# Whole-tile PSUM copies in an attention backward pass, and a reordered last stage

## The chip, the cores and the metric

One core of one Trainium2 chip runs the kernel as one program. The metric is the device time of one execution in microseconds (us). Five engines work at once and meet through semaphores: TensorE (PE; its weight loads are PEld), VectorE (DVE), ScalarE (ACT), GpSimd (POOL) and SyncE (SP), whose instructions here are only DMA issues. "SPq", "ACTq" and "POOLq" are the instruction queues of these engines where they issue DMAs or wait. Each queue runs in program order.

## The reference

The forward pass is a parallel block (attention and a gated feed-forward network on the same normalised input); the kernel returns its output and the gradients with respect to six inputs.

```python
def _A_ref(x, wqkv, wo):            # S = 2048, D = 448, H = 16, Dh = 28
    qkv = (x @ wqkv).reshape(B, S, 3, H, Dh).transpose(2, 0, 3, 1, 4)
    q, k, v = qkv[0], qkv[1], qkv[2]
    scores = jnp.einsum("bhqd,bhkd->bhqk", q, k) * (Dh ** -0.5)
    p = _softmax(scores, axis=-1)
    o = jnp.einsum("bhqk,bhkd->bhqd", p, v)
    return o.transpose(0, 2, 1, 3).reshape(B, S, D) @ wo

def _B_ref(x, w_gate, w_up, w_down):          # F = 1792
    return (_silu(x @ w_gate) * (x @ w_up)) @ w_down

x = A_x
xn = _layernorm(x, axis=-1)                   # eps = 1e-5
return x + _A_ref(xn, A_wqkv, A_wo) + _B_ref(xn, B_w_gate, B_w_up, B_w_down)
...
_out, _vjp = jax.vjp(_f, A_x, A_wqkv, A_wo, B_w_gate, B_w_up, B_w_down)
return (out, *_vjp(grad_out))                 # everything in bfloat16
```

## The kernel before

Everything is cut into 16 row tiles of 128 rows (NT = 16). Heads are padded from 28 to 32 and taken in 4 groups of 4 heads (G = 4). The program has four stages, laid out by hand; the order on each engine's queue is the order in which the Python text emits instructions, because the tile framework is told to keep it and adds only the semaphores.

**Prologue and forward stage** (0 to about 730 us): normalisation, projections, attention forward, feed-forward network forward and backward. The change doesn't touch it.

**Backward stage** (lines 777 to 858, about 730 to 1558 us). It walks over 512 units. A unit is one pair of heads (pr, 8 of them), one block of 512 keys (kc, 4), one half of the rows (w, 2) and one tile of 128 rows in that half (qi, 8). Eight units that differ only in qi make a window (UW = 8; W is its number, pos the place in it), and there are 64 windows. Iteration k of the loop does, in this order:

- PE, L798: the scores of unit k into a PSUM tile `sd` (two banks; the pool has three such tiles). PE, L811: the product dO V^T of unit k-1 into the next `sd` tile.
- ACT, L816: E[k] = exp(scores). DVE, L828: ds[k-1] = (L811's result) * E[k-1].
- ds must also be had transposed, in the tile `dsT`, for the gradient of q. For six of eight units SP issues a transposing DMA (L830). For qi = 1 and qi = 4 (TQ) PE transposes instead (`pe_transpose`, L718, eight 128x128 transposes into the PSUM tile `aux`, one bank), and `tr_out` copies the bank out: ACT the first half (L725), DVE the second (L727). The unit with qi = 1 is transposed at the end of pos 6; the one with qi = 4 at pos 0 of the next window, between L798 and L811 (`late_tr`).
- PE, L691 (`acc_mm`): the sums of dV and dK over the units, three units behind.

Spread over each window are: a job of 14 to 21 PE matmuls (the list `jobs`, lines 655 to 662; a few windows have none), emitted in four parts at pos 1 to 4 and copied out by ACT at pos 4 (`job_out`, L670); and the q gradient of two windows ago (`dq_mm`, L740, at pos 5, and `dq_out` on DVE at pos 6, L752 to L758). Transposes, job and `dq_mm` all use the one buffer of `aux`, in turn: each must wait until the one before has been copied out. Loads for later windows are put into the SP queue between the transposing DMAs (`job_load`, `load_pair`, `load_group`, `load_w`); `ds` has eight buffers, and one is free again when its transposing DMA has landed.

**Last stage** (lines 862 to 918, from about 1565 us). `dwq_mms` adds up the weight gradient of head group 3 for four chunks c of 128 input features: 32 K/V matmuls (L619, reading `dkv_sp`), then 32 q matmuls (L624, reading `dq_sp`, which arrives by a transposing DMA that SP issues last). Chunk by chunk, each into its own `sd` tile, and `dwq_out` copies each out (ACT L634, POOL L641 and L642). Then, for each row tile t, PE adds the input gradient g_ps from `pab` (L893, two partial sums of the earlier jobs) and from `dq_c` (L895, 12 matmuls), and the layer norm's backward follows: DVE copies g_ps to SBUF and sums its rows (L899), DVE multiplies it by xn and sums (L903, `junk`), two tiny DVE instructions make the coefficients bb and cc (L907, L909), ACT makes t1 (L912), DVE t2 (L914), POOL adds dy (L917), and SP stores the tile (L918). `load_c` loads `dq_c` two row tiles at a time, three loads ahead; `pab` and `dy_t` are loaded whole before the loop.

Of the kernel before, what the change touches and what calls it, by code (L numbers as in the profile page):

```python
# [18 lines left out]
D = 448  # L19
# [3 lines left out]
G = 4  # L23
# [14 lines left out]
def kernel(  # L38
# [573 lines left out]
    def dwq_mms(g, c, ps):  # L612

        out = []
        lhs = lambda t: xn_sp[:, t, c * P:(c + 1) * P]

        def kvm(t):
            for hp in range(2):
                pe.matmul(ps[:, hp * P:(hp + 1) * P], lhsT=lhs(t), rhs=dsp[2 * g + hp][0][:, t, :],  # L619
                          start=(t == 0 and hp == 0), stop=(t == NT - 1), skip_group_check=True)  # L620

        def qm(t):
            for hp in range(2):
                pe.matmul(ps[:, 256 + hp * 64:256 + hp * 64 + 64], lhsT=lhs(t),  # L624
                          rhs=dsp[2 * g + hp][1][:, t // 8, t % 4, t % 8 // 4, :],
                          start=False, stop=(t == NT - 1), skip_group_check=True)
        for f in (kvm, qm):
            out += [lambda t=t, f=f: f(t) for t in range(NT)]
        return out

    def dwq_out(g, c, ps):
        d0, dn = DCH[c]
        o = outp.tile([P, 384], BF16, name="dwq_raw")
        act.copy(out=o[:], in_=ps[:, :384])  # L634
        z = outp.tile([P, 3, 4, DH], BF16, name="dwq_z")
        kv = o[:, :256].rearrange("p (h v j r) -> p h v j r", h=2, v=2, r=HP)
        for tq in range(3):
            for hp in range(2):
                src = (o[:, 256 + 64 * hp:320 + 64 * hp].rearrange("p (j r) -> p j r", r=HP) if tq == 0
                       else kv[:, hp, 2 - tq])  # L640
                pool.tensor_copy(out=z[:, tq, 2 * hp:2 * hp + 2, :], in_=src[:, :, :DH])  # L641
        pool.dma_start(  # L642
            out=out_2[d0:d0 + dn, :].rearrange("p (t c) -> p t c", t=3)[:, :, g * 4 * DH:(g + 1) * 4 * DH],
            in_=z[:dn].rearrange("p t h d -> p t (h d)"))

    def job_mms(i, ps):
        j = jobs[i]
        if j[0] == "dwq":
            return dwq_mms(j[1], j[2], ps)
        if j[0] == "y":  # L650
# [10 lines left out]
        return [lambda n=n: pe.matmul(ps[:, :D], lhsT=t[:, n, :], rhs=w[:, n, :],  # L661
                                      start=(n == 0), stop=(n == NFC - 1)) for n in range(NFC)]
# [50 lines left out]
    def pe_transpose(W, qi):  # L713

        ds, dsT = DS[W * UW + qi], st[("dsT", W)]
        ps = ps_x.tile([P, 8, P], BF16, name="aux")
        for i in range(8):
            pe.transpose(ps[:, i, :], ds[:, i // 4, (i % 4) * P:(i % 4 + 1) * P], ident_bf[:])  # L718
        st["tr"] = (ps, dsT[:, :, :, qi * P:(qi + 1) * P])

    def tr_out(eng):

        ps, dst = st["tr"]
        if eng is act:
            act.copy(out=dst[:, 0], in_=ps[:, 0:4, :])  # L725
        else:
            dve.tensor_copy(out=dst[:, 1], in_=ps[:, 4:8, :])  # L727

    def dq_mm(W, half):
        pr, kc, w, _ = units[W * UW]  # L730
# [46 lines left out]
    for k in range(N + 2 * UW):  # L777
# [21 lines left out]
                          rhs=kv[HP * j:HP * j + HP, kc * 512:(kc + 1) * 512],  # L799
                          start=True, stop=True, tile_position=(HP * j, 0))  # L800
        late_tr = pos == 0 and 1 <= W <= NW
        if late_tr:
            pe_transpose(W - 1, TQ[1])
        if 1 <= k <= N:
            pr, kc, w, qi = units[k - 1]
            q, kv = qd[pr]
            qt = 8 * w + qi
            d_ps = ps_sd.tile([P, 2, 512], FP32, name="sd")
            for j in range(2):
                r = 64 + HP * j  # L810
                pe.matmul(d_ps[:, j, :], lhsT=q[r:r + HP, qt * P:(qt + 1) * P],  # L811
                          rhs=kv[r:r + HP, kc * 512:(kc + 1) * 512],
                          start=True, stop=True, tile_position=(r, 0))
        if k < N:
            E[k] = ework.tile([P, 2, 512], BF16, name="E")
            act.activation(out=E[k][:], in_=s_ps[:], func=ACT.Exp, scale=SCALE)  # L816
        if late_tr:
            tr_out(act)
            tr_out(dve)
        job = jobs[W] if W < len(jobs) else None  # L820
        if pos == 6 and 2 <= W <= NW + 1:
            dq_out(W - 2)
# [29 lines left out]
            job_out(W, st["aux"])  # L852
        if pos == 6 and W < NW:
            pe_transpose(W, TQ[0])
            tr_out(act)
            tr_out(dve)
    while sp_later:
        sp_later.pop(0)()
# [3 lines left out]
    with ExitStack() as fin:  # L862
# [1 line left out]
        wk = fin.enter_context(tc.tile_pool(name="wk", bufs=3))  # L864
        one = fin.enter_context(tc.tile_pool(name="one", bufs=1))
        dy_t = one.tile([P, NT, D], BF16, name="dy_t")
        act.dma_start(out=dy_t[:], in_=dy_d)
        pab = [one.tile([P, NT, D], BF16, name=f"pab{i}") for i in range(2)]
        for i, src in enumerate((pA_d, pB_d)):
            for hf in range(2):  # L870
                sp.dma_start(out=pab[i][:, 8 * hf:8 * hf + 8, :], in_=src[:, 8 * hf:8 * hf + 8, :])
        dq_c = {}

        def load_c(ck):
            if ck < NT // 2:
                dq_c[ck] = ckf.tile([P, 3 * G, 2 * P], BF16, name="dq_c")
                sp.dma_start(out=dq_c[ck][:], in_=dqkv_d[ck])
        load_c(0)
        load_c(1)
        for c in range(4):  # L880
            ps = ps_sd.tile([P, 2, 512], FP32, name="sd")
            for f in dwq_mms(3, c, ps[:, 0, :]):
                f()
            dwq_out(3, c, ps[:, 0, :])
        wq = wtile["wq"]
        for t in range(NT):
            if t % 2 == 0:
# [6 lines left out]
            for n in range(3 * G):  # L894
                pe.matmul(g_ps, lhsT=cks[:, n, (t % 2) * P:(t % 2 + 1) * P], rhs=wq[:, n, :],  # L895
                          start=False, stop=(n == 3 * G - 1))
            g_sb = wk.tile([P, D], FP32, name="g_sb")
            s1 = wk.tile([P, 1], FP32, name="s1")
            dve.tensor_scalar(out=g_sb[:], in0=g_ps, scalar1=1.0, scalar2=None, op0=ALU.mult, op1=ALU.add,  # L899
                              accum_out=s1[:])  # L900
            junk = wk.tile([P, D], FP32, name="junk")
            s2 = wk.tile([P, 1], FP32, name="s2")
            dve.scalar_tensor_tensor(out=junk[:], in0=g_sb[:], scalar=1.0, in1=xn_sp[:, t, :D],  # L903
                                     op0=ALU.mult, op1=ALU.mult, accum_out=s2[:])
            bb = wk.tile([P, 1], FP32, name="bb")
            cc = wk.tile([P, 1], FP32, name="cc")
# [43 lines left out]
```

## Time and profile before

| what | value |
|---|---|
| time, median of 3 runs | 1656.14 us (1640.88 to 1673.39) |
| the profiled execution | 1655.46 us, its span 1653.5 us |
| mean granted TensorE clock in it | 0.957 |
| busy: PE / DVE / ACT / POOL | 90% / 68% / 71% / 24% |
| backward stage, from the first E to the last | 732.0 to 1556 us |
| last stage, from the first matmul of group 3 | 1564.8 us to the end |

A page of a profile gives busy time per engine, the span in 40 slices, the chain of work that ended last, and groups of instructions with what ended the idle time before them. Busy is not the same as needed: PE's matmuls are pipelined, and their ends are modelled. A group's line reads: line, engine, operation, output<-inputs with partitions x elements, count | busy us, mean ns of one | idle time of that engine just before, and who ended it. The timeline lists instructions by start and duration, with the idle time before each in brackets.

### The profile page before, as it was taken

The numbers are of one execution on the slowest core, as the hardware profiler recorded it, in microseconds if no ns is written. First come the engines' busy times: TensorE is split into PE (matmuls) and PEld (weight loads), VectorE is DVE, ScalarE is ACT, GpSimd is POOL, SyncE is SP. The second block draws the span as 40 slices with busy tenths as digits, with TensorE's granted clock in tenths as the row PEclk, the third lists the DMA queues.
The fourth block names the chain that finished last, engine by engine and source line by source line (L and its number), as shares of the span: only waits on it lengthen the run. The fifth ranks groups of instructions, "written<-read, shape, count | busy, mean of one in ns | idle before, by whom it ended". The sixth has DMA issues, their size and how long they took to land.

```text
span 1653.5 us, 32129 instructions
## 1 busy us (share of the span) xinstructions
PE 1489.1 (90%) x12176; PEld 620.8 (38%) x12176; DVE 1130.9 (68%) x1530; ACT 1167.4 (71%) x1346; POOL 400.7 (24%) x664
## 2 busy tenths in 40 slices
PE   3699999999999999969998989999989899999884
PEld 1233333333333333323443434334345334544352
DVE  6355455655556556628887878888888788888635
ACT  2478888888878877727776777777777777877511
POOL 4133233344334435320110011110112101211132
PEclk9799999999999999979999989999999999999888
DMA  4787567776987777579999999999999999999962
GB/s 128 143 168 137 114 119 148 153 149 130 159 167 150 138 159 157 126 214 200 218 204 201 181 189 202 200 198 203 204 201 197 204 195 181 175 198 185 188 226 88
DMA packets 682155, 285.13 MB, mean 172 GB/s; under 512 B 637792, under 2 KB 651088, under 8 KB 682000
## 3 DMA queue, kind: packets, MB, share of 16 engines
q1 hardware_dynamic: 653616, 215.74, 70.5%
q0 software_dynamic: 25808, 64.30, 15.9%
q10 hardware_dynamic: 2576, 3.04, 0.6%
q8 instruction: 95, 1.56, 0.4%
q14 instruction: 60, 0.49, 0.1%
HBM read 67.34 MB, written 63.44 MB: 79 GB/s over the span
## 4 chain that ended last, share of the span: by engine, by line
PE 60%; DMA 12%; DVE 11%; ACT 8%; issue 6%; SPq 2%; POOL 1%; DVEq 0%; POOLq 0%; ACTq 0%
PE s_ps L531 9%; PE f_ps L313 8%; PE f_ps L339 8%; DMA dsT<-ds 7%; PE sd L798 5%; ACT E L816 5%; DVE ds L828 5%; PE o_ps L513 5%; PE aux L661 5%; PE acc L691 4%; PE aux L740 4%; PE aux L655 3%; PE f_ps L157 3%; PE sd L811 2%; ACT dsT L725 2%
## 5 line engine op out<-in xcount | busy, mean ns | idle before, releaser
L828 DVE TENSOR_TENSOR ds<-sd,E 128x1024 bf16<-128x1024 f32 x512 | 607.6, 1217 | 84.7 <-PE sd L811 41.0
L816 ACT ACTIVATE E<-sd 128x1024 bf16<-128x1024 f32 x512 | 520.0, 1031 | 194.6 <-PE sd L811 101.5
L535 ACT ACTIVATE eT<-s_ps 128x1024 bf16<-128x1024 f32 x512 | 497.1, 1022 | 132.0 <-PE s_ps L531 130.4
L798 PE MATMUL sd<-KV,QD 32*128 32x512 bf16 x1024 | 202.4, 392 | 19.5 <-DVE ds L828 9.2
L811 PE MATMUL sd<-KV,QD 32*128 32x512 bf16 x1024 | 203.1, 389 | 12.4 <-DVE ds L828 8.4
L691 PE MATMUL acc<-ds,Qsp 128*32 128x512 bf16 x1024 | 204.4, 395 | 1.2 <-DVE ds L828 1.2
L691 PE MATMUL acc<-E,dOsp 128*32 128x512 bf16 x1024 | 204.1, 395 | 0.0
L531 PE MATMUL s_ps<-qT,kT 32*128 32x512 bf16 x1024 | 202.1, 393 | 0.0
L339 PE MATMUL f_ps<-xnT,wgu 128*128 128x512 bf16 x448 | 122.8, 391 | 20.4 <-DMA wd<-in_B_w_down_dram 11.8
L378 POOL DMA_DIRECT2D hd_d<-fT x168 | 126.7, 767 | 39.6 <-DVE fT L363 25.9
L661 PE MATMUL aux<-W,ck 128*128 128x448 bf16 x448 | 106.6, 354 | 6.7 <-DVE dsT L727 6.7
L706 POOL DMA_DIRECT2D dqkv_d<-dkv_o x64 | 39.2, 617 | 292.1 <-ACT dkv_o L697 290.1
L531 PEld LDWEIGHTS <-kT 32*128 32x128 bf16 x1024 | 48.0, 91 | 161.2 <-issue 160.3
L798 PEld LDWEIGHTS <-QD 32*128 32x128 bf16 x1024 | 50.4, 91 | 149.4 <-issue 141.0
L513 PE MATMUL o_ps<-eT,v_sp 128*32 128x512 bf16 x1024 | 104.4, 398 | 0.0
L313 PE MATMUL f_ps<-xn_sp,f_sp 128*128 128x448 bf16 x448 | 101.6, 359 | 0.0
L727 DVE COPY dsT<-aux 128x512 bf16<-128x512 bf16 x128 | 54.3, 424 | 60.5 <-ACT dsT L725 60.3
L691 PEld LDWEIGHTS <-dOsp 128*32 128x32 bf16 x1024 | 50.4, 94 | 120.4 <-issue 117.4
L811 PEld LDWEIGHTS <-QD 32*128 32x128 bf16 x1024 | 69.4, 91 | 55.1 <-issue 36.1
L718 PE MATMUL aux<-ident_bf,ds 128*128 128x128 bf16 x1024 | 78.6, 220 | 11.7 <-DVE dq_acc L752 4.3
L351 DVE SCALAR_TENSOR_TENSOR g<-t_sb,f_ps 128x512 f32<-128x512 f32 x56 | 38.4, 686 | 72.6 <-ACT t_sb L349 72.4
L313 PEld LDWEIGHTS <-f_sp 128*128 128x128 bf16 x672 | 58.5, 98 | 73.5 <-issue 23.4
(130 smaller groups left out, 1819.1 us busy)
## 6 DMA issues: line engine op xcount, KB each, us to landing
hd_d<-fT POOLq DMA_DIRECT2D x168, 128.0 KB, 4.4
ck<-hd_d SPq DMA_DIRECT2D x32, 448.0 KB, 4.6
ck<-hd_d SPq DMA_DIRECT2D x16, 576.0 KB, 4.9
dsT<-ds SPq DMA_TRANSPOSE x384, 4.1
dq_c<-dqkv_d SPq DMA_DIRECT2D x8, 768.0 KB, 4.7
dqkv_d<-dkv_o POOLq DMA_DIRECT2D x64, 64.0 KB, 3.6
W<-wT_d SPq DMA_DIRECT2D x14, 224.0 KB, 3.5
out_dram<-dw_o POOLq DMA_DIRECT2D x28, 96.0 KB, 3.9
```

What stands on the lines that cost most here:

```text
L313: pe.matmul(acc[:, :D], lhsT=src[:, 12 * (t // 4) + 4 * wi + t % 4, :], rhs=rhs[:, t, :D], start=(t == 0), stop=(t == NT - 1))
L339: pe.matmul(st[name][:], lhsT=w(c), rhs=src[:, tsl, c, :], start=(c == 0), stop=(c == 3))
L378: pool.dma_start(out=hd_d[tsl, :, G + NFC * wi + fc, :].rearrange("k p s -> p k s"), in_=o[:, wi, :].rearrange("p (k s) -> p k s", k=4))
L513: pe.matmul(o_ps[HP * hh:HP * (hh + 1), :], lhsT=v[:, kt, HP * hh:HP * (hh + 1)], rhs=e[hh // 2][:, hh % 2, :], start=(kt == 0), stop=(kt ...
L531: pe.matmul(s_ps[:, j, :], lhsT=kT[r:r + HP, kt * P:(kt + 1) * P], rhs=qT[r:r + HP, qc * 512:(qc + 1) * 512], start=True, stop=True, tile_ ...
L535: act.activation(out=e[:], in_=s_ps[:], func=ACT.Exp, scale=SCALE)
L661: return [lambda n=n: pe.matmul(ps[:, :D], lhsT=t[:, n, :], rhs=w[:, n, :], start=(n == 0), stop=(n == NFC - 1)) for n in range(NFC)]
L691: pe.matmul(acc[r:r + HP, :], lhsT=src[:, qt, 64 * hp + HP * j:64 * hp + HP * j + HP], rhs=m[:, j, :], start=(qt == 0), stop=(qt == NT - 1 ...
L798: pe.matmul(s_ps[:, j, :], lhsT=q[HP * j:HP * j + HP, qt * P:(qt + 1) * P], rhs=kv[HP * j:HP * j + HP, kc * 512:(kc + 1) * 512], start=Tru ...
L811: pe.matmul(d_ps[:, j, :], lhsT=q[r:r + HP, qt * P:(qt + 1) * P], rhs=kv[r:r + HP, kc * 512:(kc + 1) * 512], start=True, stop=True, tile_p ...
L816: act.activation(out=E[k][:], in_=s_ps[:], func=ACT.Exp, scale=SCALE)
L828: dve.tensor_tensor(out=DS[k - 1][:], in0=d_ps[:], in1=E[k - 1][:], op=ALU.mult)
```

## The change

`tr_out` now copies the whole bank with one instruction on one engine: ACT for the unit of pos 0, DVE for the one of pos 6. The transposes at pos 0 move behind L811. In the last stage the K/V matmuls of all four chunks come before the q matmuls of all four (two chunks share an `sd` tile); `pab` and `dy_t` are loaded in quarters from within `load_c`; the row sum of g_ps is ACT's (its copy g_sb is now bfloat16 and nothing reads it), and the product with xn (DVE) and t1 (ACT) read g_ps in PSUM.

```diff
@@ dwq_mms, job_mms
-            out += [lambda t=t, f=f: f(t) for t in range(NT)]
+            out.append([lambda t=t, f=f: f(t) for t in range(NT)])
...
-            return dwq_mms(j[1], j[2], ps)
+            return sum(dwq_mms(j[1], j[2], ps), [])
@@ tr_out
-        if eng is act:
-            act.copy(out=dst[:, 0], in_=ps[:, 0:4, :])
-        else:
-            dve.tensor_copy(out=dst[:, 1], in_=ps[:, 4:8, :])
+        out, in_ = dst.rearrange("p j c q -> p (j c) q"), ps[:]
+        act.copy(out=out, in_=in_) if eng is act else dve.tensor_copy(out=out, in_=in_)
@@ the loop over units
         late_tr = pos == 0 and 1 <= W <= NW
-        if late_tr:
-            pe_transpose(W - 1, TQ[1])
         if 1 <= k <= N:
...
                 pe.matmul(d_ps[:, j, :], ...)
+        if late_tr:
+            pe_transpose(W - 1, TQ[1])
         if k < N:
             E[k] = ework.tile([P, 2, 512], BF16, name="E")
             act.activation(out=E[k][:], in_=s_ps[:], func=ACT.Exp, scale=SCALE)
         if late_tr:
             tr_out(act)
-            tr_out(dve)
...
         if pos == 6 and W < NW:
             pe_transpose(W, TQ[0])
-            tr_out(act)
             tr_out(dve)
@@ the last stage
-        act.dma_start(out=dy_t[:], in_=dy_d)
-        for i, src in enumerate((pA_d, pB_d)):
-            for hf in range(2):
-                sp.dma_start(out=pab[i][:, 8 * hf:8 * hf + 8, :], in_=src[:, 8 * hf:8 * hf + 8, :])
         def load_c(ck):
+            if ck >= NT // 2:
+                return
+            if ck % 2 == 0:
+                ts = slice(2 * ck, 2 * ck + 4)
+                for i, src in enumerate((pA_d, pB_d)):
+                    sp.dma_start(out=pab[i][:, ts, :], in_=src[:, ts, :])
+                act.dma_start(out=dy_t[:, ts, :], in_=dy_d[:, ts, :])
+            dq_c[ck] = ckf.tile([P, 3 * G, 2 * P], BF16, name="dq_c")
+            sp.dma_start(out=dq_c[ck][:], in_=dqkv_d[ck])
...
+        mms = []
         for c in range(4):
-            ps = ps_sd.tile([P, 2, 512], FP32, name="sd")
-            for f in dwq_mms(3, c, ps[:, 0, :]):
-                f()
-            dwq_out(3, c, ps[:, 0, :])
+            if c % 2 == 0:
+                g_t = ps_sd.tile([P, 2, 512], FP32, name="sd")
+            mms.append((g_t[:, c % 2, :], dwq_mms(3, c, g_t[:, c % 2, :])))
+        for part in range(2):
+            for c, (ps, m) in enumerate(mms):
+                for f in m[part]:
+                    f()
+                if part == 1:
+                    dwq_out(3, c, ps)
...
-            g_sb = wk.tile([P, D], FP32, name="g_sb")
+            g_sb = wk.tile([P, D], BF16, name="g_sb")
-            dve.tensor_scalar(out=g_sb[:], in0=g_ps, scalar1=1.0, scalar2=None, op0=ALU.mult, op1=ALU.add,
-                              accum_out=s1[:])
+            act.activation(out=g_sb[:], in_=g_ps, func=ACT.Identity, accum_out=s1[:])
-            dve.scalar_tensor_tensor(out=junk[:], in0=g_sb[:], scalar=1.0, in1=xn_sp[:, t, :D],
+            dve.scalar_tensor_tensor(out=junk[:], in0=g_ps, scalar=1.0, in1=xn_sp[:, t, :D],
-            act.activation(out=t1[:], in_=g_sb[:], func=ACT.Identity, scale=rstd[:, t:t + 1], bias=bb[:, 0:1])
+            act.activation(out=t1[:], in_=g_ps, func=ACT.Identity, scale=rstd[:, t:t + 1], bias=bb[:, 0:1])
```

More of the change, by code (lines that the diff above doesn't have):

```diff
@@ L866 @@
         dy_t = one.tile([P, NT, D], BF16, name="dy_t")
-        act.dma_start(out=dy_t[:], in_=dy_d)
         pab = [one.tile([P, NT, D], BF16, name=f"pab{i}") for i in range(2)]
-        for i, src in enumerate((pA_d, pB_d)):
-            for hf in range(2):
-                sp.dma_start(out=pab[i][:, 8 * hf:8 * hf + 8, :], in_=src[:, 8 * hf:8 * hf + 8, :])
         dq_c = {}
         def load_c(ck):
-            if ck < NT // 2:
-                dq_c[ck] = ckf.tile([P, 3 * G, 2 * P], BF16, name="dq_c")
-                sp.dma_start(out=dq_c[ck][:], in_=dqkv_d[ck])
+            if ck >= NT // 2:
[7 more added lines that the diff above has]
+            sp.dma_start(out=dq_c[ck][:], in_=dqkv_d[ck])
         load_c(0)
         load_c(1)
+        mms = []
         for c in range(4):
-            ps = ps_sd.tile([P, 2, 512], FP32, name="sd")
-            for f in dwq_mms(3, c, ps[:, 0, :]):
-                f()
-            dwq_out(3, c, ps[:, 0, :])
+            if c % 2 == 0:
[7 more added lines that the diff above has]
+                    dwq_out(3, c, ps)
         wq = wtile["wq"]
```

## The prediction

> **What bounds the kernel now.** I began with the page's engine shares (PE 90%, ACT 71%, DVE 68%), which are averages over stages with different limits, and so cut the span into stretches: here two windows of the backward stage without and with a disturbance, one without a job, and the loop of the last stage. Columns: stretch and length; busy us (instructions) of PE, PEld, DVE, ACT, POOL; granted clock; DMA share; GB/s.
>
> ```profile
> 1371.90:1383.90 12.00, 11.75 (x113) 4.89 (x110) 10.67 (x12) 9.26 (x12) 1.78 (x3) 1.00 1.04 175
> 1191.30:1206.60 15.30, 11.92 (x115) 5.22 (x112) 10.83 (x12) 9.34 (x13) 0.56 (x1) 1.00 1.10 202
> 1383.90:1397.30 13.40, 11.76 (x98) 4.25 (x96) 10.86 (x12) 9.60 (x12) 1.19 (x2) 0.75 0.93 186
> 1587.40:1645.00 57.60, 44.49 (x222) 21.72 (x222) 38.89 (x112) 12.15 (x16) 17.49 (x20) 0.92 0.35 113
> ```
>
> A quiet window takes 12.0 to 12.25 us (12.6 with the longer "y" jobs), PE nearly always busy, DVE 10.7. Taking the start of every eighth L816 from the timeline, some 40 of 64 windows are quiet; in 18 (12.4 to 16.5 us) DVE waited for transposing DMAs; in a few without a job the clock fell. Next, the chain of waits of a quiet window, the groups and the waits of the stage:
>
> ```profile
> 1053.92 0.20 PE sd L811 x2
> 1054.12 1.28 ACT E L816 x2
> 1055.40 0.54 issue
> 1055.94 0.61 ACT dsT L725
> 1056.55 0.02 issue
> 1056.58 0.44 DVE dsT L727
> 1057.01 0.04 issue
> 1057.06 0.92 PE aux L661 x4
> ...
> L727 DVE COPY dsT<-aux 128x512 bf16<-128x512 bf16 x128 | 54.3, 424 | 60.5 <-ACT dsT L725 60.3
> ...
> DVE ds L828 <- DMA dsT<-ds: 32.7, 30, 2.9
> ```
>
> The chain is PE's through most of the window, then for 3.1 us (1053.92 to 1057.06) ACT and DVE: two exponentials, ACT's half copy, DVE's half copy, and only then the job may take `aux`. The group says that DVE's half waits for ACT's half though they write different halves: 0.95 us a window. Last, the last stage in the timeline:
>
> ```profile
> 1574.08 0.96 PE L624 MATMUL sd<-dq_sp,xn_sp 128*128 128x64 bf16 x15 [5.54 <-DMA dq_sp<-dq_o]
> ...
> 1587.37 4.06 PE L895 MATMUL sd<-W,dq_c 128*128 128x448 bf16 x12 [2.42 <-DMA dq_c<-dqkv_d]
> ...
> 1592.14 0.62 DVE L903 SCALAR_TENSOR_TENSOR junk<-g_sb,xn_sp 128x448 f32<-128x448 f32 x1
> ...
> 1597.53 0.62 DVE L899 TENSOR_SCALAR_CACHE_REDUCE g_sb<-sd 128x448 f32<-128x448 f32 x1
> ...
> 1598.18 1.02 DVE L903 SCALAR_TENSOR_TENSOR junk<-g_sb,xn_sp 128x448 f32<-128x448 f32 x1
> ```
>
> PE stands idle 5.54 us for `dq_sp`, and the first row tile is complete only at 1591.4, since `dq_c` lies behind all of `pab` and `dy_t`. Then DVE sets the pace: its L899 starts every 3.31 us, while PE needs 2.65 from one L893 to the next. The last POOL add ends at 1645.0; 8.5 us follow that the change leaves alone.
>
> **The change, part by part: backward stage.** Removed per window: two half copies on ACT (587 ns each) and two on DVE (424). Added: one whole copy on each. Neither is in the trace. ACT: L816 takes 1.02 us for 1024 columns from the same memory; bounds 0.59 (one half) and 1.19 (two); I take 1.02. DVE: a 32-bit cast takes 0.62 for 448 columns (L323) and 0.69 for 512 (L166), so some 0.19 is fixed; 0.19 + 2 x (0.42 - 0.19) = 0.66; bounds 0.42 and 0.85.
>
> At pos 6 DVE's copy follows ds directly (before it waited 0.2 for ACT): 0.2 less and 0.24 more, no change. ACT loses a copy, so E of pos 7 starts some 0.15 earlier. At pos 0 DVE has neither wait nor copy: 0.77 + 0.34, so the next ds starts 1.1 us earlier. That matters because L798 of pos 2 waits for this ds (three `sd` tiles): before, its ds ran 1056.92 to 1058.1 and L798 stood ready at 1057.9.
>
> Against that, L811 now comes first at pos 0 and waits for E of pos 7, a wait that the transposes used to fill. With the starts of the window above: L798 at 1054.37, E done 1055.0, L811 to 1055.37, transposes (0.55) to 1055.92, ACT's copy 1055.98 to 1057.0, job at 1057.04, before 1057.06. Queued behind the longer ACT copy is E of pos 1, 0.5 later, which L811 of pos 2 awaits: 1058.0, before 1058.18. From there I carried PE, ACT and DVE on with the row durations: the job's second part 0.19 earlier, `dq_mm` 0.3, the transposes of pos 6 0.45, L798 of pos 7 0.46 (8.11 us after the job's start, before 8.57); from there to the next job 3.47 against 3.52. So a quiet window becomes 12.1 - 0.5 = 11.6. If the ACT copy takes 1.19, 0.35 is left; with both copies at their low ends, 0.8.
>
> The 18 windows with DMA waits I give nothing: there SP issues back to back (a transposing DMA every 1.3 us, loads 0.6), and a window that asks for six, a `dkv_sp` and four loads needs 7.8 + 1.3 + 2.4 and whatever the queue holds back. Sum: 40 x 0.5 = **20 us**; ends: a loss of 13 (0.2 in each of 64, if the later E is not covered) and a gain of 38 (0.6 in each).
>
> **Last stage, start.** The K/V matmuls of c = 1 to 3 (1.79 us each, the pitch of L619 to L624 at 1578.97) go into the idle time from 1568.1: they end at 1573.4; four q parts of 0.93 end at 1577.2. Their cover is the transposing DMA of `dq_sp`, issued 1565.63, landed 1574.0 behind 1792 KB of `dy_t`; with 448 KB ahead of it, 1571. The loads ahead of the first `dq_c` shrink from 5376 to 1344 KB; at the 410 GB/s of these slices it lands near 1575 (before 1587.3). So row tile 0 is complete at 1577.2 + 2.65 = 1579.9 instead of 1591.4. At the slow clock (3.34 us per 32, the row at 1574.86) it would be 1585.
>
> A rule of the Trainium skill bears on this. The granted clock is 0.65 over 1560 to 1574, and 32 K/V matmuls take 3.34 us after the 5.54 us of idling and 1.95 later. "TensorE: Matmul & The Clock Gate" (Part 1) says that an idle window of about 3.4 us halves the clock and as long a busy one restores it; by it K/V matmuls without a pause would run fast from the second chunk on, as I assumed from the rows.
>
> **Last stage, loop.** Off DVE: L899 (0.62 and its 0.08 read). To ACT: a sum pass over 448 columns; its accumulate form is not in the trace. L670 moves 448 columns in 0.53, L912 in 0.76; bounds 0.53 and 0.84, I take 0.6. t1 from PSUM: 0.53 to 0.76, 0.65. L903 took 0.62 alone and 1.02 beside POOL's add; L899, reading PSUM, 0.62 beside it, so 0.62 here; bound 1.02. In the order of the changed kernel L903 waits for ACT's sum, so both count. One cycle: ACT's sum 0.05 + 0.6, to DVE 0.07, L903 0.6, bb 0.11, to ACT 0.19, t1 0.65: 2.3 us; with all high ends 3.0. PE's 2.65 lies between and becomes the pace.
>
> "PSUM — Partial Sum Buffer" (PSUM bank collisions raise a hardware error) speaks against this part: two engines must not touch one bank at once, reads included. The row is the 0.95 us above. Without the rule the cycle would be some 0.65 shorter; since PE sets the pace, the sum is the same.
>
> Moved on the queues: per four row tiles two `pab` issues of 0.33 on SP, behind the stores, and a `dy_t` issue of 0.39 on ACT, covered by ACT's slack of 0.35 per tile (cost without it 1.2 in all). `dq_c` now waits behind the `pab` quarters, for t = 8 and 12; and POOL, which after the q parts must first copy and store four chunks (some 12 us, to 1588), adds its first dx late, so that SP's next load is late for t = 6. I allow 3 us of PE waits, 0 to 6. End of the last add: 1579.9 + 15 x 2.65 + 3 + 4.0 (sum, L903, t1, t2, add) = 1626.6, against 1645.0: **18 us**; ends 12 (pace 2.8, start 1580) and 22.
>
> Sum, against the profiled execution's own time: 1655.5 - 20 - 18 = **1617** (that time is 0.7 below the median of the runs). A difference under 2%, 33 us, can hardly be told from none here, so the line is 1623.
>
> **Rivals.**
> 1. *The windows don't get shorter, because SP's queue and the DMAs set them.* For it: DMA share 1.00 to 1.10 almost everywhere, 18 windows that already wait on landings, and faster units need the same six transposing DMAs in less time. Against it: quiet windows with and without job loads take the same 12.0 to 12.25, and landings there return to 3.2 us. Only the last stage gains: 1655.5 - 18 = 1637.
> 2. *Slower: PE's clock.* The wait now left open at L811 of pos 0 (0.3 us a window) costs the granted clock, as in the windows without a job (0.74 and 0.75 in two of them). At 0.75 a window with 11.6 us of PE work takes 15.5, 3.4 more. It is slower by 2% from (33 + 18) / 3.4 = 15 windows on; 20 give 1655.5 + 68 - 18 = 1706. Against it: the disturbed window above has 3 us of PE waits and clock 1.00.
> 3. *More than I count*: DMA windows gain as well and nothing waits in the last stage: 1655.5 - 38 - 22 = 1595.
>
> **How the numbers follow.** Forecast 0.58, its own range 1603 to 1631; rival 1 0.27; rival 2 0.05; rival 3 0.10. The range 1594 to 1646 takes in rivals 1 and 3 and leaves out rival 2. Faster by over 2%: three quarters of the forecast, rival 3, a little of rival 1: 0.56. Slower is rival 2, 0.05; the rest is 0.39.
>
> **What would show it.** Right: L725 as x64 on each engine, ACT near 1.02 and DVE near 0.66; DVE's wait for ACT gone; quiet windows near 11.6; the 5.54 us before L624 gone; first L895 near 1577.5; L893 every 2.65 us. Wrong: quiet windows still at 12; more DVE time waiting for transposing DMAs than 33 us; a clock under 1.00 in windows with jobs; L893 at 2.9 or more, with ACT or DVE named before it.

## The result, and the profile after

| | before | changed |
|---|---|---|
| median (20 runs each) | 1651.43 us | 1634.51 us |
| ratio, with its 95% interval | | 0.9896 [0.9875, 0.9916] |
| the profiled execution: time, span | 1655.5, 1653.5 us | 1634.7, 1632.6 us |
| mean granted clock in it | 0.957 | 0.960 |

The changed kernel is about 17 us (1.0%) faster, in the profiled executions 20.9. The forecast was 38 us, of which the backward stage was to give 20 and the last stage 18. By the starts of every eighth exponential (L816 before, L814 after) and the ends in the last stage, the two profiled executions differ like this:

| part | before | after | difference | forecast |
|---|---|---|---|---|
| 60 windows with a job | 771.8 us | 765.8 | -6.0 | -20 |
| 4 windows without a job | 52.3 | 46.6 | -5.6 | 0 |
| end of the last exponential to row tile 0 complete | 35.3 | 28.9 | -6.4 | -11.5 |
| from there to the end of the last add | 53.5 | 51.0 | -2.5 | -6.9 |

Every part that was forecast to move moved in the forecast's direction. The windows with a job, on which most hung, gave less than a third (and even that is within the spread of two executions, as the first experiment shows). The windows without a job, for which the forecast had nothing, gave almost as much. First the same four kinds of stretch as before the change, in the same order: a quiet window, a disturbed one, one without a job, the loop of the last stage (stretch and length; busy us and instructions of PE, PEld, DVE, ACT, POOL; granted clock; DMA share; GB/s).

```profile
1343.40:1355.10 11.70, 11.44 (x110) 4.85 (x110) 10.54 (x11) 9.34 (x11) 0.56 (x1) 1.00 1.07 192
1188.40:1204.80 16.40, 12.38 (x112) 5.30 (x111) 11.43 (x11) 9.52 (x12) 0.56 (x1) 0.90 1.00 208
1379.00:1389.90 10.90, 9.09 (x96) 3.55 (x96) 10.38 (x11) 9.24 (x11) 1.20 (x2) 1.00 1.20 206
1570.20:1624.10 53.90, 45.38 (x231) 22.43 (x227) 28.64 (x80) 21.69 (x49) 20.65 (x31) 0.91 0.53 176
```

Start to start, quiet windows alternate between 11.78 and 12.05 us (12.00 and 12.23 before): 0.2 shorter, not 0.5. The disturbed window is longer than the one shown before. The window without a job took 13.40 at a granted clock of 0.75 before and takes 10.90 at 1.00 now. In the last stage DVE is down to 28.6 us busy, as meant.

The copies themselves (duration in ns: minimum, median, maximum), and two groups of the waits (us in total, times, longest):

```profile
L725 DVE COPY dsT<-aux x64: 678/679/692, 749.9 to 1543.1; 128x1024 bf16<-128x1024 bf16 x64
L725 ACT COPY dsT<-aux x64: 1012/1012/1014, 752.0 to 1544.5; 128x1024 bf16<-128x1024 bf16 x64
...
DVE ds L825 <- DMA dsT<-ds: 45.7, 34, 3.9
...
PE sd L807 <- ACT E L814: 23.7, 75, 0.7
```

The copies cost what the forecast priced (0.66 and 1.02). The 60 us in which DVE waited for ACT's half copy are gone. In their place stand 13 us more of DVE waits for transposing DMAs (32.7 before), and a wait of PE for the exponential at L807, the second product: 23.7 us (2.1 before, when it was L811). The chain of waits across the end of a quiet window shows where it sits:

```profile
1353.85 0.34 PE sd L796 x2
1354.19 0.02 issue
1354.22 1.03 ACT E L814
1355.25 0.04 issue
1355.29 0.39 PE sd L807 x2
1355.68 0.57 PE aux L718 x8
1356.25 0.02 issue
1356.27 1.02 ACT dsT L725
1357.29 0.04 issue
1357.33 0.73 PE aux L661 x3
```

The exponential of pos 7, the product that waits for it, the transposes, ACT's copy and the job follow each other with nothing between them: 3.12 us from that exponential's start to the job (L661). Before the change it was 2.94, two half copies included.

### The profile page after: what moved, and what is told of

Same layout as the page of the kernel before. It is cut to its first block, busy times and chain, and to the rows that moved or that the text cites. A ratio compares the mean times of both kernels' runs of the same rounds, so it can differ in the third digit from the quotient of the medians.

```text
span 1632.6 us, 32026 instructions
## 1 busy us (share of the span) xinstructions
PE 1462.6 (90%) x12176; PEld 610.3 (37%) x12176; DVE 1112.0 (68%) x1434; ACT 1181.5 (72%) x1314; POOL 401.8 (25%) x664
## 4 chain that ended last, share of the span: by engine, by line
PE 64%; DMA 12%; ACT 8%; DVE 7%; issue 4%; SPq 3%; POOL 1%; DVEq 0%; POOLq 0%; ACTq 0%
PE s_ps L531 9%; PE f_ps L313 8%; DMA dsT<-ds 7%; PE f_ps L339 7%; PE sd L796 5%; ACT E L814 5%; PE aux L661 5%; PE o_ps L513 4%; PE acc L691 4%; PE aux L718 3%; PE aux L738 3%; PE aux L655 3%; DVE ds L825 3%; ACT dsT L725 3%; PE f_ps L157 3%
## 5 line engine op out<-in xcount | busy, mean ns | idle before, releaser
L814 ACT ACTIVATE E<-sd 128x1024 bf16<-128x1024 f32 x512 | 516.5, 1024 | 186.7 <-PE sd L807 136.0
L807 PE MATMUL sd<-KV,QD 32*128 32x512 bf16 x1024 | 201.7, 387 | 25.6 <-ACT E L814 23.7
L661 PE MATMUL aux<-W,ck 128*128 128x448 bf16 x448 | 106.8, 355 | 3.6
L796 PEld LDWEIGHTS <-QD 32*128 32x128 bf16 x1024 | 50.7, 91 | 155.5 <-issue 147.5
L718 PE MATMUL aux<-ident_bf,ds 128*128 128x128 bf16 x1024 | 79.8, 221 | 11.1 <-DVE dq_acc L750 5.7
L807 PEld LDWEIGHTS <-QD 32*128 32x128 bf16 x1024 | 65.0, 91 | 64.1 <-issue 59.1
L313 PEld LDWEIGHTS <-f_sp 128*128 128x128 bf16 x672 | 58.6, 99 | 73.5 <-issue 23.7
L738 PE MATMUL aux<-dsT,Ksp 128*32 128x512 bf16 x1024 | 75.2, 391 | 6.9 <-DMA dsT<-ds 5.4
```

Source lines behind the costliest of these rows:

```text
L313: pe.matmul(acc[:, :D], lhsT=src[:, 12 * (t // 4) + 4 * wi + t % 4, :], rhs=rhs[:, t, :D], start=(t == 0), stop=(t == NT - 1))
L796: pe.matmul(s_ps[:, j, :], lhsT=q[HP * j:HP * j + HP, qt * P:(qt + 1) * P], rhs=kv[HP * j:HP * j + HP, kc * 512:(kc + 1) * 512], start=Tru ...
```

## Experiments

### One half of the change at a time

The first kernel takes the backward stage's edits alone, the second the last stage's alone.

> The changed backward stage with the old last stage. Theory (most of the backward gain I forecast was never there: a quiet window loses 0.2 us, not 0.5, and the windows with DMA waits nothing): quiet windows 11.78 and 12.05 us as in the changed kernel, backward stage 8 to 14 us shorter than before, time 0.5 to 0.8% below before. Rival (the last stage's new loads and waits ate the backward gain): the backward stage brings 18 us or more here, over 1%.

> The old backward stage with the changed last stage. Theory: from the first matmul of group 3 to the last add 74 us instead of 80, 8 to 12 us less in the time (0.5 to 0.7%), with the PE waits for dq_c and pab at the ninth and thirteenth row tile there again. Rival (the wait for dq_sp and the late end of the backward stage belong to the backward change): 15 us or more here.

| kernel | median us | ratio to before | first to last exponential | last exponential to last add |
|---|---|---|---|---|
| before | 1651.37 | | 824.1 us | 88.8 us |
| backward stage only | 1646.34 | 0.9959 [0.9924, 0.9995] | 811.6 | 88.4 |
| last stage only | 1633.61 | 0.9889 [0.9825, 0.9954] | 816.7 | 73.9 |
| both (the change) | 1634.51 | 0.9896 [0.9875, 0.9916] | 812.4 | 80.0 |

(The ratio of the last row is from its own comparison.) The backward edits bring some 7 us, the last stage's some 18, as much as the whole change; the intervals leave room for 6 and 11 us either way. That is close to the prediction's rival 1 (windows not shorter, 1637).

These two kernels also profile the old and the new windows a second time. The 60 windows with a job took 765.1 us in both, the new windows of the first kernel and the old ones of the second (771.8 and 765.8 in the pair above). The four without a job took 46.5 new and 51.5 old (46.6 and 52.3). So the 6.0 us of the windows with a job are no more than one execution of the same old windows differs from another; what both pairs show is the 5 to 6 us of the windows without a job, which run at a higher granted clock (see rival 2 below).

The last column adds something the forecast had no term for: the same last stage took 73.9 us behind the old windows and 80.0 behind the new ones. All of that lies ahead of row tile 0, which was complete 22.5 us behind the last exponential, against 28.9.

### The order of the transposes, and who copies which bank

Two kernels with whole copies. In the first the transposes of pos 0 stand ahead of the second product, as before the change:

```diff
         late_tr = pos == 0 and 1 <= W <= NW
+        if late_tr:
+            pe_transpose(W - 1, TQ[1])
         if 1 <= k <= N:
...
-        if late_tr:
-            pe_transpose(W - 1, TQ[1])
         if k < N:
```

> The changed kernel with the transposes of pos 0 put back between the score matmuls and the dO V^T matmuls; the whole copies stay. Theory A (the moved transposes open a wait of PE for the exponential and take back what the copies gave): quiet windows at 11.5 or less, PE's wait for E before the second matmuls gone, 10 us or more below the changed kernel. Theory B (the chain is exponential, exponential, ScalarE's copy of 1.01 us, job, and ScalarE is free no earlier either way): quiet windows unchanged within 0.1 us, time within 4 us of the changed kernel.

In the second the engines change places: DVE copies the bank of pos 0, ACT that of pos 6.

```diff
         if late_tr:
-            tr_out(act)
+            tr_out(dve)
...
             pe_transpose(W, TQ[0])
-            tr_out(dve)
+            tr_out(act)
```

> The changed kernel with the engines of the two whole copies exchanged: VectorE (0.68 us) copies at pos 0, ScalarE (1.01 us) at pos 6. Theory B (ScalarE's copy between two exponentials is what ends the chain before the job): the copy at pos 0 starts as the transposes end and is 0.33 us shorter, and E of pos 1 is no longer behind it; quiet windows 11.3 to 11.6, 12 to 20 us below the changed kernel where DMA waits allow. Rival (VectorE is then late again at pos 0 and L796 of pos 2 waits for its ds, as before the change): quiet windows at 11.8 or more, no gain.

With the old order the quiet windows are 11.55 and 11.82 us, 0.23 shorter than in the changed kernel and 0.43 shorter than before. The chain at the end of such a window, in that kernel:

```profile
1364.86 0.32 PE sd L796 x2
1365.18 0.55 PE aux L718 x8
1365.73 0.34 PE sd L809 x2
1366.07 0.04 DVEq L825
1366.11 0.04 DVE ds L825
1366.15 1.01 ACT dsT L725
1367.15 0.04 issue
1367.20 0.92 PE aux L661 x4
```

The transposes run while ACT is busy with the exponentials of pos 7 and 0, so that the bank is ready when ACT comes to it, and the copy follows at once. From the start of the exponential of pos 7 to the job it is 2.90 us, against 3.12. So the whole copies are worth 0.43 us a quiet window, and the moved transposes take half of it back: the two edits of one change pull against each other.

And yet the time hardly follows: 1636.64 us, ratio 0.9872 [0.9818, 0.9925], not to be told from the changed kernel, and 810.8 us from first to last exponential instead of 812.4 (810.3 to 811.6 in the runs `e1_backward_only`, `e7_one_input` and `e12_wq_late`, which have the changed kernel's windows). DVE's waits for transposing DMAs grew to 56.6 us.

The swapped kernel refuted what I expected of it: 1651.29 us, 0.9966 [0.9926, 1.0006], quiet windows 12.25 and 12.53 by turns. The two waits of its profile that tell why:

```profile
PE sd L807 <- ACT E L814: 56.5, 71, 1.1
DVE ds L825 <- DMA dsT<-ds: 6.6, 7, 2.8
```

ACT's copy at pos 6 stands in ACT's queue ahead of the exponential of pos 7, for which the product of the next window waits: what I had hoped to gain at pos 0 is lost there. The second line is the more useful one. The longest windows of these kernels have the fewest waits for DMAs, the shortest have the most:

| kernel | quiet windows of 18 to 62, mean | DVE's waits for dsT | all 44 windows with a job from 18 to 62 | of it, beyond 44 quiet ones |
|---|---|---|---|---|
| engines swapped | 12.41 us | 6.6 us | 553.7 us | 8 us |
| before | 12.14 | 32.7 | 553.7 | 20 |
| the same windows, in "last stage only" | 12.14 | 20.8 | 550.5 | 16 |
| changed | 11.95 | 45.7 | 550.2 | 25 |
| the same windows, in "backward stage only" | 11.93 | 38.3 | 549.2 | 24 |
| transposes ahead again | 11.79 | 56.6 | 549.6 | 31 |

(Quiet: under 12.4 us, under 12.6 for the swapped kernel.) A window that gets 0.35 us shorter, over 44 windows 15 us, shortens their sum by 1 to 4. The rest comes back in the disturbed ones, as the last column shows.

### What sets the disturbed windows: bytes, SP's queue, or their distribution?

Adding up the durations of SP's DMA issues in the timeline, SP issues for some 11 us of a quiet window (11.1 before, 10.9 after), and for 12.8 to 12.9 us of a disturbed one. A transposing DMA takes 1.29 us of it at the median and up to 4.7. Three kernels ask what fills it. The first asks for the same loads on POOL's queue:

```diff
-        return [lambda i=i, dst=dst, r0=r0, src=src: sp.dma_start(
+        return [lambda i=i, dst=dst, r0=r0, src=src: pool.dma_start(
... (so in load_group, job_load and load_w)
```

> The changed kernel, with every load of the backward stage (hd_d, x, weights, pairs, groups) issued on POOL's queue, so that SP's queue holds only transposing DMAs. Theory A (SP's queue: a transposing DMA takes 1.3 us of it and a load 0.4 to 0.6 and up to 4 behind it): DVE's waits for the landing of dsT fall from 45.7 us to under 20, the wait of 5.4 us before the last q gradient goes, the backward stage (812 us in the profile of the changed kernel) becomes 800 to 806, and the kernel 8 to 14 us faster than the changed one. Theory B (the DMA engines themselves are full, so it doesn't matter who asks): DVE's waits stay between 35 and 55 us and the time is within 5 us of the changed kernel, ratio to before 0.987 to 0.993.

It is slower: 1695.1 us, ratio 1.0263 [1.0218, 1.0308]; the backward stage takes 879.5 us. Neither theory said that. Quiet windows are what they were (11.78 and 12.05), but eight windows from 18 to 62 take 19 us at the mean. The worst, in the timeline (start, duration, engine, line; in brackets the idle time before):

```profile
1315.60 16.78 SPq L827 DMA_TRANSPOSE dsT<-ds  x2
...
1327.59 1.23 DVE L825 TENSOR_TENSOR ds<-sd,E 128x1024 bf16<-128x1024 f32 x1 [9.24 <-DMA dsT<-ds]
```

Two transposing DMAs, with no load left in SP's queue, take 16.78 us to issue. So it is not the number of SP's issues that binds: an issue itself can stretch, from 1.29 us at the median to 8.4 each here. That the loads had been paced by the transposing DMAs between them, and on a queue of their own run all at once, is my reading; no run separates it from another. POOL's queue is also of another kind than SP's (as the loads moved, the page's `software_dynamic` queue went from 64.3 to 109.5 MB and its `hardware_dynamic` one from 215.7 to 170.5), and the loads were not tried on ACT's. "DMA: Bandwidth & Descriptors" (Queues, rings and completion order) in the Trainium skill says that each DMA engine takes the queues that have work in turn, a packet at a time; the stretched issue would fit that, but no run here shows the turns.

The same with the transposes ahead again, as the windows are shortest there:

> As the one before, and the transposes of pos 0 stand before the second product again, as in the kernel before (whole copies kept). That order alone gave quiet windows of 11.55 us instead of 11.78, and DVE waits for landings of 57 us instead of 46. Theory A: with SP's queue freed the shorter window is kept in the sum: quiet windows 11.55, DVE waits under 25, backward stage 795 to 800 us, 15 to 20 us faster than the changed kernel. Theory B: the waits grow again to over 50 us and the backward stage stays at 806 to 812.

1707.34 us, ratio 1.0339 [1.0277, 1.0402], quiet windows 11.56, DVE's waits 102.2 us: the same, from another side.

The second kernel takes bytes away and leaves every issue. It loads one chunk of `hd_d` for each job and leaves out the others, so its y and dx are not the reference's; it is there for its time alone:

```diff
-            sp.dma_start(out=t[:], in_=hd_d[j[1], :, :G + NFC, :])
+            sp.dma_start(out=t[:, :1], in_=hd_d[j[1], :, :1, :])
...
-        return [lambda n=n: pe.matmul(ps[:, :D], lhsT=t[:, n, :], rhs=w[:, n, :],
+        return [lambda n=n: pe.matmul(ps[:, :D], lhsT=t[:, 0, :], rhs=w[:, n, :],
```

> The changed kernel; each job's load of hd_d brings one of its 18 or 14 chunks, and the job's matmuls all read that one, so that 424 or 416 KB less are loaded in each of 48 windows, with as many DMA issues as before (the output leaves these chunks out). Theory A (in the disturbed windows the DMA engines are full of bytes): DVE's waits for landings of dsT fall from 45 us to under 25, the windows of over 12.3 us become fewer, and the backward stage takes 795 to 805 us instead of 812. Theory B (it is the number and the order of SP's issues): waits of 35 to 50 us and 808 to 814 us.

```profile
DVE ds L825 <- DMA dsT<-ds: 11.7, 11, 3.7
...
DMA packets 682777, 285.11 MB, mean 175 GB/s; under 512 B 637904, under 2 KB 651200, under 8 KB 682624
DMA packets 682777, 262.57 MB, mean 164 GB/s; under 512 B 644048, under 2 KB 657344, under 8 KB 682624
```

(The last two lines are the changed kernel and this one: as many packets, 22.5 MB less, or 544 KB for each y job, where the expectation has 424, and 416 for each dx job.) DVE's waits fall from 45.7 to 11.7 us, the backward stage from 812.4 to 788.2, the median to 1611.63 (ratio to before 0.9747 [0.9695, 0.98]). Quiet windows stay at a mean of 11.95, and what the 44 windows take beyond quiet ones falls from 25 us to 14. So a quiet window is the engines' chain, and a disturbed one is in good part a matter of bytes, not of the number of issues or packets.

The third kernel (put on the combination at the end of this section) spreads the loads of pairs and groups over twice as many windows:

```diff
-                for lst, n in ((pload, 2), (gload, 1), (wload, 2)):
+                for lst, n in ((pload, 1), (gload, W % 2), (wload, 2)):
```

> The combination of the run before (transposes ahead of the second product, early loads in the last stage, one-input bb and cc, q parts 0, 2, 1, 3), with the loads for the next pair and group of heads spread: one load of a pair per window instead of two (eight windows instead of four), and one load of a group in every second window instead of every one. As many bytes and issues as before, fewer of them in one window. Theory A (a window is disturbed when the bytes asked for in it go beyond what the DMA engines move in its time): what the disturbed windows take beyond a quiet one falls from 30 us to 15 to 22, and the time is 5 to 12 us below the 1626 of the combination. Theory B (what is asked for later is only waited for later): the excess stays at 25 to 33 us and the time at 1620 to 1630.

1624.51 us, ratio 0.9826 [0.9791, 0.9862]. What the 44 windows take beyond quiet ones is 33 us, against 32 in the combination without it; DVE's waits are 53.7 against 55.4. That is theory B. My reading is that there is no window to move the bytes to, as SP already issues for 10.9 us of a quiet window's 11.8.

### The weights ahead of the last transposing DMAs

Why did the last stage start later behind the last exponential (11.6 us instead of 8.7)? After the change PE waits here for the last transposed units (5.37 us below, 3.8 to 5.0 in four more executions with these windows; 1.8 before):

```profile
1553.93 1.89 PE L738 MATMUL aux<-dsT,Ksp 128*32 128x512 bf16 x14 [5.37 <-DMA dsT<-ds]
1555.75 2.53 PE L619 MATMUL sd<-dkv_sp,xn_sp 128*128 128x128 bf16 x22
```

and in SP's queue the two loads of wq stand ahead of the last windows' DMAs. One kernel asks for them behind these:

```diff
+        if k == N + 1:
+            for f in load_w("wq", 2):
+                f()
...
-                if W == len(jobs) - 1:
-                    wload.extend(load_w("wq", 2))
```

> The changed kernel; the two loads of the weights wq (688 KB each), which stand in SP's queue in window 62 ahead of the last twelve transposing DMAs, are issued behind the last of these. Theory A (what the shorter windows won was lost again at the end of the stage, where SP, held up by these loads, is late with its transposing DMAs): PE's wait of 5.4 us before the last q gradient falls to 1 to 2 us, the K/V matmuls of the last stage start 8 to 9 us after the last exponential instead of 11.6, and window 63 takes about 11 us instead of 12.5; 3 to 4 us shorter, if the later weights don't hold the first row tile. Theory B (the wait is the latency of the DMA itself): the wait stays over 4 us, and the time is that of the changed kernel or, with the weights late, 2 to 5 us longer.

```profile
1559.11 1.42 PE L738 MATMUL aux<-dsT,Ksp 128*32 128x512 bf16 x14 [2.20 <-DMA dsT<-ds]
```

The wait falls from 5.37 to 2.20 us and L619 starts 8.0 us behind the last exponential, so these loads have a large part in the late start. They don't make it alone: in the combination below, where they stand as before, the wait was 1.05 us. Row tile 0 is complete 26.4 us behind the last exponential instead of 28.9. The time shows none of it: 1638.65 us, ratio 0.9894 [0.9844, 0.9944]; 2.5 us is less than this comparison can tell. (One of its six executions took 3052.81 us, which nothing here explains.)

### The loop of the last stage

The forecast of the loop had a pace of 2.65 us, 3 us of waits and a tail of 4.0. The changed kernel's timeline:

```profile
1582.03 1.03 POOL L921 TENSOR_TENSOR dx<-t,dy_t 128x448 bf16<-128x448 f32 x1 [1.57 <-DVE t L918]
1582.41 0.67 DVE L911 SCALAR_TENSOR_TENSOR bb<-s,rstd 128x1 f32<-128x1 f32 x1
1583.00 0.14 DVE L913 SCALAR_TENSOR_TENSOR cc<-s,rstd 128x1 f32<-128x1 f32 x1
1584.00 0.69 DVE L918 SCALAR_TENSOR_TENSOR t<-xn_sp,cc,t 128x448 f32<-128x448 bf16 x1 [0.85 <-ACT t L916]
...
1586.73 0.69 DVE L918 SCALAR_TENSOR_TENSOR t<-xn_sp,cc,t 128x448 f32<-128x448 bf16 x1 [0.85 <-ACT t L916]
...
1593.53 0.35 PE L898 MATMUL sd<-pab,ident_bf 128*128 128x448 bf16 x1 [1.75 <-DMA pab<-pB_d]
1595.91 4.66 PE L900 MATMUL sd<-W,dq_c 128*128 128x448 bf16 x12 [2.04 <-DMA dq_c<-dqkv_d]
```

Row tile follows row tile by 2.65 us in 13 of 15 steps; the two steps at row tiles 8 and 9 are 8.98 and 2.91, 6.6 us too long, for loads. And L911, which makes 128 numbers out of 256, takes 0.67 us instead of 0.15: it ends with POOL's add. DVE's own cycle is thereby 2.73 us (L918 to L918), and the chain falls 0.08 a row tile behind PE. Two kernels:

```diff
         def load_c(ck):
... (the second quarter of pab ahead of dq_c(2); the third and fourth, and dy's, right behind it)
```

> The changed kernel; in the last stage the quarters of pab and dy are asked for as early as the first row tiles (the second quarter ahead of the third dq_c, the third and fourth right behind it), so that none waits in SP's queue behind the stores. Theory A (the loads were asked for too late): the waits at row tile 8 (1.75 + 2.04 us of PE, 5.8 of ACT) go, and the loop from the first finished row tile to the last add takes 45 to 48 us instead of 51. Theory B (the memory gives no more than some 200 to 280 GB/s there): the waits move to row tiles 4 to 8, and the loop stays at 49 to 52.

Every step is 2.65 us, all waits for loads are gone, and the loop takes 45.7 us instead of 51.0 (6.6 us of waits less, and a tail 1.3 longer, as the chain is no longer let catch up). Theory A. As a time it is unresolved: 1634.11 us, ratio 0.990 [0.986, 0.994].

```diff
+        nrs = one.tile([P, NT], FP32, name="nrs")
+        dve.tensor_scalar(out=nrs[:], in0=rstd[:], scalar1=-1.0 / D, scalar2=None, op0=ALU.mult)
...
-            dve.scalar_tensor_tensor(out=bb[:], in0=s1[:], scalar=-1.0 / D, in1=rstd[:, t:t + 1],
-                                     op0=ALU.mult, op1=ALU.mult)
+            dve.tensor_scalar(out=bb[:], in0=s1[:], scalar1=nrs[:, t:t + 1], scalar2=None, op0=ALU.mult)
```

(and cc in the same way)

> The changed kernel; the two tiny DVE instructions that make bb and cc take the factor -rstd/D as a scalar made ahead of the loop, so that each reads one tensor in SBUF (and a scalar) instead of two. Theory A (a DVE instruction that reads two tensors in SBUF is held until POOL's add ends): bb returns from 0.54 to 0.67 us to about 0.15, the step from one g_ps to the next falls from 2.73 to PE's 2.65, and the loop is 1.0 to 1.5 us shorter. Rival (POOL's add holds every DVE instruction that reads SBUF): bb stays over 0.5 and the step at 2.73.

```profile
1577.54 0.68 DVE L918 SCALAR_TENSOR_TENSOR t<-xn_sp,cc,t 128x448 f32<-128x448 bf16 x1 [0.80 <-ACT t L916]
...
1578.30 1.03 POOL L921 TENSOR_TENSOR dx<-t,dy_t 128x448 bf16<-128x448 f32 x1 [1.57 <-DVE t L918]
...
1579.06 0.21 DVE L913 TENSOR_SCALAR bb<-s,nrs 128x1 f32<-128x1 f32 x1
...
1580.18 0.68 DVE L918 SCALAR_TENSOR_TENSOR t<-xn_sp,cc,t 128x448 f32<-128x448 bf16 x1 [0.80 <-ACT t L916]
```

With one tensor read, bb takes 0.21 us beside the same add, and DVE's cycle is 2.64 (1577.54 to 1580.18). So it is the second tensor operand in SBUF that was held: L907, a SCALAR_TENSOR_TENSOR like bb but with one operand in PSUM, takes 0.62 us beside the add. "SBUF — State Buffer" (SBUF: two separate sides) says that DVE and GpSimd share a port pair that one holds for a whole instruction, and counts a DVE instruction with two SBUF inputs in; here that is 0.5 us on an instruction of 0.15. My expectation named the wrong quantity, though: the step from one g_ps to the next had been PE's 2.65 already. What is gained is the tail behind the last row tile: 4.2 us, against 4.7 in the changed kernel and 6.0 in the run before, where no wait of PE lets the chain catch up. The loop took 46.1 us (its waits for loads happened to be 2.2), the median was 1630.93, ratio 0.9878 [0.9828, 0.9928].

### The combination

Transposes ahead again, early loads, one-input bb and cc, and the q parts in the order 0, 2, 1, 3, so that a chunk's matmuls don't wait for ScalarE's copy of the other bank in the same tile.

> The changed kernel with the transposes of pos 0 ahead of the second product again, the last stage's loads issued early, bb and cc with one tensor input each, and the q parts of the four chunks in the order 0, 2, 1, 3. If the gains add up as their profiles show them (quiet windows 11.55 instead of 11.78, some 8 us less what the landings take back; loop 44 to 45 us instead of 51; 1.2 us of PE waits for ScalarE's copies at the start), it is 8 to 14 us faster than the changed kernel: ratio to before 0.981 to 0.985. If the landings set the backward stage, only the last stage's 5 to 8 us are seen: 0.984 to 0.987.

1626.18 us, ratio 0.9843 [0.9793, 0.9894]. The last stage from the last exponential to the last add is 66.8 us (80.0 in the changed kernel), the loop 44.9; the backward stage, with 55.4 us of DVE waits, is 809.3 against 812.4. The last stage's gain adds up, the windows' doesn't. Some of the 66.8 is chance: with the spread loads the wait ahead of the K/V matmuls was 4.5 us again instead of 1.1, and the last stage took 71.2. That kernel is the fastest of those that compute everything (1624.51 us; its interval ends at 0.9862, just below where the changed kernel's begins), though not to be told from the combination.

## Why the prediction was wrong, point by point

**Direction and prices right.** Each copy cost what the rows gave (0.68 and 1.01 us for 0.66 and 1.02), DVE's wait for ACT went, the 5.54 us before L624 went (L624 waits no more for `dq_sp`), and PE's 2.65 us became the pace of the loop.

**The step that failed: "a quiet window becomes 12.1 - 0.5 = 11.6", times 40.** It failed in the size of the gain and in what a gain is worth.

The size was 0.2, not 0.5. The forecast had 0.46 of it in the middle of the window, from the job's start to L798 of pos 7 ("8.11 us after the job's start, before 8.57"). This stretch takes 8.23 and 8.50 us by turns, against 8.48 and 8.70: 0.20 to 0.25 less. The job's second part came 0.2 earlier, as forecast, but `dq_mm` (0.3 forecast) and the transposes of pos 6 (0.45) gained no more than that. The stretch from there to the next job, "3.47 against 3.52", takes 3.55. In the kernel that leaves the transposes ahead the middle is the same and this stretch is 3.32: the move cost 0.23 us, the wait at L807 that the transposes used to fill, and the forecast booked it at nothing, as it compared the job's time only with the kernel before (1057.04 for 1057.06). That this other kernel has 11.55 and 11.82, near the forecast's 11.6, is luck: its middle was put 0.25 too short at the mean, and its end 0.15 too long.

Then the worth. "The 18 windows with DMA waits I give nothing" took it that a quiet window's gain stays. With 0.35 us less per quiet window 44 windows gained 1 to 4 us: what they take beyond quiet ones grew from 16 or 20 us (two executions) to 31. It is also what shrinks when bytes are taken away. Rival 1 named this (SP's queue and the DMAs set the windows) and gave 1637 for 1634.5, in part by luck: it counted 18 us for the last stage, which gave 8.9 in the profiled pair, and nothing for the windows without a job. I weighed it at 0.27, on the ground that quiet windows with and without job loads take the same time. That shows only that a quiet window doesn't wait. Nor does the DMA share of 1.00 to 1.10, which I put down for the rival, tell the two apart: in the changed kernel it is 1.07 at the mean of the quiet windows and 1.06 at that of the disturbed ones. What differs is the bytes that were moved, 2.3 MB a window against 2.8.

**Last stage, start: -6.4 for -11.5.** Of the 5.1 us that are missing, 2.9 are the later start of the K/V matmuls behind the last exponential, in which the wq loads have a large part (shown). Two waits of 0.6 us for ScalarE, as two chunks share a tile, were not in the sum. The K/V matmuls took 9.2 us instead of 8.6, at a mean granted clock of 0.77 behind the wait of 5.37; behind the old windows, where the wait was 1.4, they took 7.2 at 1.00. "410 GB/s of these slices" was too much for the burst of `pab`, `dy_t` and `dq_c` (the 4.2 MB that SP asked for first, from 1558.1 on, had landed at 1573.3, some 280 GB/s), but no row tile ahead of number 8 waited for it.

**Last stage, loop: -2.5 for -6.9.** The pace was right. "I allow 3 us of PE waits" measured 6.6 (8.98 + 2.91 less two steps of 2.65), at row tile 8, and 4.0 for the tail measured 4.7. In other profiled executions of the same last stage the waits were 3 to 7 us, so the term is one of chance as well as of size; with the early loads they were 0, 0.9 and 1.4 us in three kernels.

**Rival 2 had the sign wrong.** I feared that the wait at L807 would cost the clock. In the four windows without a job the granted clock went up: 0.74 to 0.86 before, 0.74, 0.86, 1.00 and 1.00 after, 5.6 us in all that no step counted. Of nine profiled kernels with these copies, unswapped, and the loads on SP's queue, eight have two or three of the four at 1.00 and one (early loads, profiled at 1652.44 us) has none; before, with only the last stage changed, and with the engines swapped, none of the four is. Why a window with the same matmuls keeps its clock in one order and not in another was not tried and stays open.

## What to carry to other kernels

Before a gain per iteration is multiplied by the number of iterations, look at the iterations that already wait, and for what: here for landings, in the windows that move the most bytes, and most of what the quiet windows won came back in these. A share of busy time doesn't answer that: the DMA share was the same in windows that waited and in windows that didn't. When a change holds two edits, price each against the kernel without it: the moved transposes ate half of what the whole copies gave a quiet window, and only undoing one showed it. Profile a stage more than once before a few us of it are put down to an edit: the same 60 old windows took 771.8 and 765.1 us. Loads that stand between other DMAs in one queue don't gain from another queue for the sake of a shorter one: here POOL's made the kernel 2.6% slower, and fewer bytes made it 2.5% faster, where the whole change made 1.0%.

## What the hardware showed that I had not expected

- Moving the loads to POOL's queue made the issue of transposing DMAs slower: it rose from a mean of 1.5 us to 1.8, with one pair at 16.8 us, and the kernel by 2.6%.
- A DVE instruction that reads two tensors in SBUF ends with POOL's add: 0.67 us for one of 0.15. With one tensor and a scalar it is 0.21, and `junk`, reading one operand in PSUM, took 0.62 beside the add (with both in SBUF 1.02 before).
- The granted clock of a window without a job (9.1 us of PE's time at 1.00) was 0.74 in one order of the copies and 1.00 in another; why stays open.
- ScalarE's accumulating pass is 0.54 us for 448 columns, as without it, and reading the sum out takes 0.19 more.
